# The output-weight requests of a recurrent-memory kernel: from two queues to one, two of them earlier

## The chip, the cores and the metric

The kernel runs on one core of one Trainium2 chip. The metric is the device time of one execution, in microseconds (us). A core has a matrix engine (TensorE, PE in the profile; PEld is its weight load), a vector engine (VectorE, DVE), a scalar engine (ScalarE, ACT), GpSimd (POOL) and SyncE (SP). ACT and SP can both issue transfers (DMA). The instruction that issues one stands in the program of its engine like any other, so what comes after it on that engine starts after it.

## What is computed

Two branches read the same `x` (2048 rows of 512) and are mixed by a gate per row.

```python
# A: 64 segments of 32 rows, one after another; 8 rows of memory pass from each to the next
h = concatenate([mem, xs])                       # 40 rows of 512
q, k, v = h @ Wq, h @ Wk, h @ Wv                 # 32 heads of 128: each weight is 512 x 4096
o = softmax(mask(q @ k.T * scale)) @ v
o = einsum('bhte,hed->btd', o, Wo)               # Wo: 32 heads x 128 x 512
mem, out = o[:8], o[8:]
# B: 4 blocks of 512 rows, 32 heads of 16: causal attention plus a running memory of phi(k) v
# result = g * a + (1 - g) * b,  g = sigmoid((x * gate_w).sum(-1))
```

All inputs are bf16. Wk, Wq, Wv and Wo of branch A have 4 MB each. The segments of A are a recurrence: a segment can't end before its product with Wo, and the next one needs the memory rows from it.

## The kernel before, in words

The program is planned in Python. `Prog` collects, for each engine, a list of instructions in order, with the dependences between them, and `emit` turns these into semaphore waits. An engine runs its list in order. A dependence on a DMA waits for the whole group that the DMA belongs to (`val = 16 * (d.group.base + d.group.count)`, L193): whoever reads Wo waits for all eight of its requests.

There are two stages. The first is the projection of branch B, `b_projections` (L614): 64 pieces, called one after another in the loop of `build` (L371 to L392). Each piece is a product on PE into one bank of PSUM, its eviction by ACT or DVE, and stores of the result to scratch memory in HBM, issued from SP by `store` (L626, issued at L627). The last fourteen pieces, 50 to 63, are those of block 3: keys and queries in turn, a memory product, then four pieces of V (59 to 62), evicted by ACT into `V17` (L679), and a flush. Between the pieces, `plan_loads` hands out requests for the weights of branch A from ACT (L508): twelve of 1 MB, one after each piece n with n % 5 == 2, so the last (of Wv) comes after piece 57. The SP queue holds, in order: the loads of x and of the B weights, then the stores of the pieces as they are made, and a few loads for the attention of B.

`wo_load(q)` (L518) requests heads 4q to 4q+3 of Wo: 512 KB in 512 rows of 1 KB. There are eight. In the kernel before, four come from ACT, after pieces 58, 59, 60 and 61, and four from SP after the last piece:

```python
        if n in (58, 59, 60, 61):
            v.wo_load(n - 58)
    for q in range(4, 8):
        v.wo_load(q)
```

The place of Wo in SBUF held `x` before (`v.x_sb = v.Wo_sb[:, 0:NTT, :]`, L291), so the first four requests also wait for the transposes that read x, which end at 33 us.

The second stage is `plan_a` (L933): 64 segments in groups of four. Before the first one come the eight units of `left_units(0)` (L988), which project the last 8 rows of each of four segments: KL, QL and VL in two halves each (PE at L966), an eviction and a transpose by ACT and DVE, then two turns back on PE (L1022). Then `segment(0)`: Q, K and V (L966), scores, softmax and the product with V (L1211 to L1287), and `wo` (L1302), which calls `out_part` (L1038; PE at L1044), the first reader of Wo. The order inside a segment is written out by hand in `A_ORDER` (L914). Attention of B, loads for it and the tails (mixing and output) fill the gaps. `wob_load` (L523) requests the output weights of B, woB, in eight pieces of 64 KB from SP, planned in segment 1; with nothing to wait for, SP issues them right after Wo.

The evictions of V in the pieces 59 to 62 stand on ACT between the Wo requests. The banks that they free are those into which the first products of `left_units(0)` go.

Of the kernel before, what the change touches and what calls it, by code (L numbers as in the profile page):

```python
# [220 lines left out]
def bass_gated_mix__memory_aug_recurrent_mem_tr__memory_aug_infini_attn__prompt_kernel(  # L221
    nc, A_x, A_mem0, A_Wq, A_Wk, A_Wv, A_Wo, A_seg_len, B_x, B_wq, B_wk, B_wv, B_wo, B_beta, gate_w, out, dbg=None,
):
    with ExitStack() as es:
        build(nc, es, A_x, A_mem0, A_Wq, A_Wk, A_Wv, A_Wo, B_wq, B_wk, B_wv, B_wo, B_beta, gate_w, out, dbg)


def build(nc, es, A_x, A_mem0, A_Wq, A_Wk, A_Wv, A_Wo, B_wq, B_wk, B_wv, B_wo, B_beta, gate_w, out, dbg=None):
    v = NS()
# [86 lines left out]
    def Rs(name):  # L316
        if name not in R:
            R[name] = Res(name)
            home = v.home(name)
            if home:  # L320
                R[name].readers = over(home)
        return R[name]
# [48 lines left out]
    for n in range(len(pieces)):  # L371
        if n in (8, 20, 32):
            x_chunk(v, (n + 4) // 12)
        if n == 9:
            sigmoid(v, v.beta_sb[:, :], v.gB_sb, v.omgB_sb, "gB", [Rs("beta")])
            for src, dst, res in ((v.gB_sb, v.gBp, "gB"), (v.omgB_sb, v.omgBp, "omgB")):
                for j in range(4):
                    q = slice(32 * j, 32 * j + 32)
                    P.op("gp", lambda g, src=src, dst=dst, q=q, j=j: g.tensor_copy(dst[q, :], src[q, :].rearrange("p (f j) -> p f j", j=4)[:, :, j]),
                         reads=[Rs(res)], writes=[Rs(res + "p")], name="%sp%d" % (res, j))  # L380
            v.late_const()
        if n >= 36 and n % 2 == 0 and gates:
            gates.pop(0)()
        pieces[n]()
        if n == len(pieces) - 3:
            v.late_mask()
        if n in (36, 38, 40, 42):
            bat.load(0, n // 2 % 2, "kv"[n // 40])
        if weights and n % 5 == 2:
            weights.pop(0)()  # L390
        if n in (58, 59, 60, 61):
            v.wo_load(n - 58)  # L392
    for q in range(4, 8):
        v.wo_load(q)


# [87 lines left out]
def plan_loads(v, A_x, A_mem0, A_Wq, A_Wk, A_Wv, B_wq, B_wk, B_wv, B_wo, B_beta, gate_w):  # L484
    P, Rs, C, M = v.P, v.Rs, v.C, v.M
    xsrc = A_x[0].rearrange("(i p) d -> p i d", p=128)

    def ld(grp, dst, src, res, name):
        P.dma(P.group(grp), lambda s: s.dma_start(dst, src), writes=[Rs(res)], name=name)

    def x(k):
        for h in range(2):
            o = 4 * k + 2 * h
            ld("x%d%d" % (k, h), v.x_sb[:, o:o + 2, :], xsrc[:, o:o + 2, :], "x_sb%d%d" % (k, h), "dma_x%d%d" % (k, h))
    x(0)
    for nm, dst, src in (("wk", v.wkB, B_wk), ("wq", v.wqB, B_wq), ("wv", v.wvB, B_wv)):
        ld("b" + nm, dst[:, :, :], src.rearrange("(c p) n -> p c n", p=128), nm + "B", "dma_" + nm)
    x(1)
    g = P.group("small")
    for fn, res in ((lambda s: s.dma_start(v.beta_sb[:, :], B_beta.rearrange("(o n) -> o n", o=1).to_broadcast([128, v.HB])), "beta"),  # L500
                    (lambda s: s.dma_start(v.gwr_sb[0:C, :], gate_w.rearrange("(c p) -> c p", p=128)), "gwr"),
                    (lambda s: s.dma_start(v.mem0_sb[0:M, :], A_mem0[0]), "mem0")):
        P.dma(g, fn, writes=[Rs(res)], name="dma_" + res)
    x(2)
    x(3)

    def weight(grp, dst, src, res, c):
        P.dma(grp, lambda s: s.dma_start(dst[:, c, :], src[c * 128:(c + 1) * 128].rearrange("p h e -> p (h e)")),  # L508
              writes=[Rs(res)], name="dma_%s%d" % (res, c), eng="act")
    pend = []  # L510
    for res, dst, src in (("Wk", v.Wk_sb, A_Wk), ("Wq", v.Wq_sb, A_Wq), ("Wv", v.Wv_sb, A_Wv)):
        grp = P.group(res)
        for c in range(C):
            pend.append(lambda grp=grp, dst=dst, src=src, res=res, c=c: weight(grp, dst, src, res, c))
    grp = P.group("Wo")
    wosrc = v.A_Wo.rearrange("h e d -> e h d")

    def wo(q):  # L518
        P.dma(grp, lambda s: s.dma_start(v.Wo_sb[:, 4 * q:4 * q + 4, :], wosrc[:, 4 * q:4 * q + 4, :]),
              writes=[Rs("Wo")] + ([Rs("x_sb%d%d" % (q, h)) for h in range(2)] if q < 4 else []), name="dma_Wo%d" % q, eng="act" if q < 4 else "sp")  # L520
    v.wo_load = wo

    def wob():  # L523
        grp = P.group("bwo")
        rows = B_wo.rearrange("(f g j d) n -> g j d f n", f=C, g=2, j=4)
        for j in range(4):
            for g in range(2):
                o = 32 * j + 16 * g
                P.dma(grp, lambda s, j=j, g=g, o=o: s.dma_start(v.woB_sb[o:o + 16, :, :], rows[g, j]), writes=[Rs("woB")], name="dma_woB%d%d" % (j, g))
    v.wob_load = wob  # L530
    return pend


def x_chunk(v, k):

    P, Rs, BK, C = v.P, v.Rs, v.BK, v.C
    for h in range(2):
        bk = BK.take()
        tiles = (4 * k + 2 * h, 4 * k + 2 * h + 1)

        def f(pe, bk=bk, tiles=tiles):
            ins = None
            for n, i in enumerate(tiles):
                for c in range(C):
                    o = (n * C + c) * 128
                    ins = pe.transpose(v.pb16[bk][:, o:o + 128], v.x_sb[:, i, c * 128:(c + 1) * 128], v.ident[:, :])
            return ins
        P.op("pe", f, reads=[Rs("x_sb%d%d" % (k, h)), Rs("ident")], writes=[v.rbank[bk]], name="xtr%d_%d" % (k, h))
        t0 = 128 * tiles[0]
        dst = v.xT[:, :, t0:t0 + 256].rearrange("p c (n t) -> p n c t", t=128)  # L550
        src = v.pb16[bk][:, 0:1024].rearrange("p (n c t) -> p n c t", n=2, c=C)
        for n in range(2):
            v.evac("dve" if h else "act", dst[:, n, :, :], src[:, n, :, :], [bk], [Rs("xT%d_%d%d" % (k, h, n))], "xev%d_%d%d" % (k, h, n))
        BK.give(bk)
# [6 lines left out]
def sigmoid(v, src, g, o, res, reads):  # L561

    P, rg = v.P, v.Rs(res)
    P.op("act", lambda a: a.activation(g[:, :], src, ACT.Exp, scale=-1.0), reads=reads, writes=[rg], name=res + "_e")
    P.op("dve", lambda d: d.tensor_scalar(g[:, :], g[:, :], 1.0, None, op0=ALU.add), reads=[rg], writes=[rg], name=res + "_a")
    P.op("dve", lambda d: d.reciprocal(g[:, :], g[:, :]), reads=[rg], writes=[rg], name=res + "_r")
    P.op("dve", lambda d: d.tensor_scalar(o[:, :], g[:, :], -1.0, 1.0, op0=ALU.mult, op1=ALU.add), reads=[rg], writes=[v.Rs("om" + res)],
         name="om" + res)
# [906 lines left out]
```

## Time and profile before

| | us |
|---|---|
| median of 3 runs | 927.47 |
| lowest, highest | 926.53, 928.67 |
| the profiled execution: its own time | 927.84 |
| its span, first to last instruction | 926.1 |
| busy: PE, DVE, ACT, POOL | 856.1, 651.3, 590.7, 247.1 |
| DMA: moved in all | 51.36 MB |
| DMA rate in the first three 40ths of the span | 333, 403, 372 GB/s |

The profile is one execution; its time is that of the span and of what lies around it. "Busy" is the time in which at least one instruction of the engine runs. In a timeline, SPq and ACTq are the sequencers of SP and ACT issuing a DMA; the length beside such a line is the time that issuing took, not that of the transfer. The time to landing is counted from the issue. A bracket such as `[4.27 <-ACT V L357]` says that the engine was idle for 4.27 us before this instruction and that an ACT instruction writing V at line 357 ended it; `<-issue` means that nothing the profile shows ended it. The granted clock (PEclk) is 1.00 when PE has its full clock.

### The profile page before, as it was taken

Reading aid. Unit: us, or ns where it says so; the run is one execution under the profiler, and the core shown is the slowest. Engines: PE = TensorE matmul, PEld = TensorE weight load, DVE = VectorE, ACT = ScalarE, POOL = GpSimd, SP = SyncE. Lnnn points to the kernel's source line nnn. Section 1 sums busy time; section 2 is a strip of 40 time slices with the busy share of each in tenths; the row PEclk is TensorE's granted clock in tenths of the full one; section 3 lists DMA queues with packets and bytes.
Section 4 is the critical chain, followed back from the end, with each engine's and each line's share of the span. In section 5 each row is a group of like instructions: output and inputs, shape, how many; then the busy total and the mean of one; then the engine's idle time right before and its main releaser. Section 6 shows DMA issues by size and latency. Waiting matters only on the chain. (4 is left out here: it accounts for less than half of the span.)

```text
span 926.1 us, 51464 instructions
## 1 busy us (share of the span) xinstructions
PE 856.1 (92%) x23047; PEld 442.0 (48%) x23054; DVE 651.3 (70%) x1505; ACT 590.7 (64%) x1287; POOL 247.1 (27%) x556
## 2 busy tenths in 40 slices
PE   8979989998999999999999999999999989999886
PEld 4534444444444444444445454544454445444443
DVE  4745757676676868677677777767677777868664
ACT  5745667666666676666666666666666666666453
POOL 3601222222222322223222232223322232222110
PEclk9999999999999999999999999999999999999999
DMA  9996000000011011101011111100011101000010
GB/s 333 403 372 186 13 12 17 25 12 18 16 22 43 23 44 33 33 6 28 19 20 37 28 48 33 27 15 21 22 33 39 39 21 44 17 21 4 26 44 19
DMA packets 63813, 51.36 MB, mean 55 GB/s; under 512 B 34272, under 2 KB 60008, under 8 KB 62056
## 3 DMA queue, kind: packets, MB, share of 16 engines
q1 hardware_dynamic: 59752, 33.38, 12.9%
q10 hardware_dynamic: 3840, 14.68, 4.1%
q8 instruction: 181, 2.97, 1.3%
q14 instruction: 40, 0.33, 0.1%
HBM read 33.47 MB, written 14.57 MB: 52 GB/s over the span
## 5 line engine op out<-in xcount | busy, mean ns | idle before, releaser
L818 ACT ACTIVATE PT<-ps 128x1024 bf16<-128x1024 f32 x160 | 163.2, 1020 | 32.4 <-PE ps L804 31.4
L825 POOL TENSOR_SCALAR_AFFINE_SELECT PT<-PT 128x512 bf16<-128x512 bf16 (+1 forms) x96 | 75.8, 789 | 265.9 <-ACT PT L818 255.8
L966 PE MATMUL ps<-Wv_sb,hT 128*32 128x512 bf16 x2048 | 139.2, 379 | 0.0
L966 PE MATMUL ps<-Wq_sb,hT 128*32 128x512 bf16 x2048 | 136.2, 380 | 1.3 <-ACT hT L357 0.8
L966 PE MATMUL ps<-Wk_sb,hT 128*32 128x512 bf16 x2048 | 135.4, 379 | 0.0
L1044 PE MATMUL ps<-Wo_sb,OT_sb 128*32 128x512 bf16 x2048 | 122.1, 380 | 0.0
L1265 POOL TENSOR_TENSOR P_sb<-P_sb,R_sb 128x64 bf16<-128x64 bf16 x128 | 53.6, 419 | 236.5 <-PE ps L1219 130.8
L357 ACT ACTIVATE OT_sb<-ps 128x320 bf16<-128x320 f32 x192 | 76.7, 434 | 52.5 <-PE ps L1287 38.4
L359 DVE CAST V_sb<-ps 128x512 bf16<-128x512 f32 x128 | 87.7, 685 | 24.1 <-PE ps L966 19.9
L978 DVE STREAM_TRANSPOSE QT_sb<-QN_sb 128x256 f32<-128x256 f32 x128 | 56.3, 440 | 50.5 <-ACT QN_sb L357 50.2
L357 ACT ACTIVATE QN_sb<-ps 128x512 bf16<-128x512 f32 x128 | 77.0, 601 | 21.5 <-PE ps L966 19.4
L966 PEld LDWEIGHTS ps<-Wk_sb,hT 128*32 128x32 bf16 x2048 | 53.9, 97 | 52.8 <-issue 2.3
L359 DVE CAST WH<-ps 128x256 bf16<-128x256 f32 x128 | 53.7, 420 | 31.7 <-PE ps L1044 29.7
L1228 ACT ACTIVATE P_sb<-ps 128x224 bf16<-128x224 f32 x128 | 45.7, 357 | 40.8 <-DVE QT_sb L978 17.5
L1044 PEld LDWEIGHTS ps<-Wo_sb,OT_sb 128*32 128x32 bf16 x2048 | 50.3, 96 | 44.5
L966 PEld LDWEIGHTS ps<-Wq_sb,hT 128*32 128x32 bf16 x2048 | 47.9, 96 | 47.8 <-ACT hT L357 15.5
L978 DVE STREAM_TRANSPOSE KT_sb<-KN_sb 128x256 f32<-128x256 f32 x128 | 56.1, 438 | 15.5 <-ACT KN_sb L357 13.0
L1252 ACT ACTIVATE R_sb<-ps 128x160 f32<-128x160 f32 x128 | 39.0, 305 | 40.9 <-PE ps L1245 40.9
L804 PE MATMUL ps<-QTj,KTj 32*128 32x256 bf16 (+1 forms) x768 | 62.3, 254 | 1.3 <-ACT aT_st L357 1.3
L1259 DVE TENSOR_TENSOR P_sb<-P_sb,R_sb 128x160 bf16<-128x160 bf16 x128 | 42.4, 332 | 29.8 <-ACT R_sb L1255 18.5
L1275 PE MATMUL ps<-P_sb,V_sb 32*128 32x40 bf16 x2048 | 35.3, 178 | 30.1 <-DVE P_sb L1259 14.1
L357 ACT ACTIVATE LN_sb<-ps 128x512 bf16<-128x512 f32 (+1 forms) x96 | 50.4, 525 | 13.6 <-DVE LN_sb L1055 8.8
(136 smaller groups left out, 1552.5 us busy)
## 6 DMA issues: line engine op xcount, KB each, us to landing
Wk_sb<-in_A_Wk_dram ACTq DMA_DIRECT2D x4, 1024.0 KB, 8.2
scr_kqd<-stgk SPq DMA_DIRECT2D x16, 256.0 KB, 8.7
Wq_sb<-in_A_Wq_dram ACTq DMA_DIRECT2D x4, 1024.0 KB, 7.9
Wv_sb<-in_A_Wv_dram ACTq DMA_DIRECT2D x4, 1024.0 KB, 7.7
scr_vd<-V SPq DMA_DIRECT2D x16, 136.0 KB, 6.6
Vj<-scr_vd SPq DMA_DIRECT2D x32, 68.0 KB, 2.4
Wo_sb<-in_A_x_dram SPq DMA_DIRECT2D x8, 256.0 KB, 6.8
KTj<-scr_kqd SPq DMA_DIRECT2D x128, 16.0 KB, 1.7
```

The source lines that it names most:

```text
L357: P.op("act", lambda a: a.activation(dst, src, ACT.Copy), reads=[v.rbank[k] for k in bks], writes=dres, name=name)
L359: P.op("dve", lambda d: d.tensor_copy(dst, src), reads=[v.rbank[k] for k in bks], writes=dres, name=name)
L804: ins = pe.matmul(v.pb[bks[x]][:, 256 * e + o:256 * e + o + w], KT[e][r, 128 * kc:128 * (kc + 1)], QT[r, q0:q0 + w], start=True, stop=True ...
L818: P.op("act", lambda a: a.activation(pt[:, :, :], v.ps[:, bks[0]:bks[1] + 1, :], ACT.Exp, scale=v.SCALE_B), reads=[v.rbank[b] for b in bks ...
L825: P.op("gp", lambda g: g.affine_select(mv, mv, [[0, mv.shape[1]], [1, 128]], ALU.is_ge, 0.0, base=0, channel_multiplier=-1), reads=[rp], w ...
L966: ins = pe.matmul(pb[bk][SEG * j:SEG * (j + 1), :], lhs(c), cols(w, j) if split else w[:, 512 * j:512 * (j + 1)], start=(c == 0), stop=(c ...
L978: P.op("dve", lambda d: d.transpose(to, src), reads=reads, writes=writes, name=name)
L1044: ins = pe.matmul(pb[bk][SEG * j:SEG * (j + 1), :], lhs(4 * k + j), Wo_sb[:, 4 * k + j, :], start=(first and k == ks[0]), stop=False, skip ...
L1228: P.op("act", lambda a: a.activation(P_sb[:, b, :], pb[bk][:, 0:224], ACT.Exp, scale=SCALE), reads=[rbank[bk]], writes=[Rs("P%d" % b), Rs( ...
L1252: P.op("act", lambda a: a.activation(R_sb[:, b, :], pb[bk][:, 224:384], ACT.Ln), reads=[rbank[bk]], writes=[Rs("R%d" % b)], name="ln%d_%d" ...
L1259: P.op("dve", lambda d: d.tensor_tensor(wide(P_sb, b)[:, :, 0:L], wide(P_sb, b)[:, :, 0:L], R_sb[:, b, :].rearrange("p (i q) -> p i q", q= ...
L1265: P.op(ENG["n"], lambda d: d.tensor_tensor(left(P_sb), left(P_sb), grp04(R_sb[:, b, :]), ALU.mult), reads=[Rs("R%d" % b)], writes=[Rs("P%d ...
```

## The change

All eight requests for Wo come from SP. Two of them are made between the pieces, after pieces 56 and 59; the other six after the last piece. ACT issues none.

```diff
-        if n in (58, 59, 60, 61):
-            v.wo_load(n - 58)
-    for q in range(4, 8):
+        if n in (56, 59):
+            v.wo_load((n - 56) // 3)
+    for q in range(2, 8):
         v.wo_load(q)
...
     def wo(q):
         P.dma(grp, lambda s: s.dma_start(v.Wo_sb[:, 4 * q:4 * q + 4, :], wosrc[:, 4 * q:4 * q + 4, :]),
-              writes=[...], name="dma_Wo%d" % q, eng="act" if q < 4 else "sp")
+              writes=[...], name="dma_Wo%d" % q)
```

`P.dma` issues from SP unless told otherwise. In SP's order the first request stands between the store of the third query piece of block 3 (issued at 58.96 us before) and the next store (60.67); the second stands after the store issued at 63.20 and before the last three stores of V. The other six follow the last store of V, and the eight requests of woB follow them.

## The prediction

> **What bounds the kernel now.** I first read two rows of the page: its 40 slices, 23.2 us each, of PE (TensorE) and of the DMA engines.
>
> ```profile
> PE   8979989998999999999999999999999989999886
> ...
> DMA  9996000000011011101011111100011101000010
> ```
>
> DMA is full in the first 80 us and nearly idle afterwards, and PE is full almost everywhere. So from the first segment on the program is a dense chain on PE, and a shift of its start carries to the end. Only the first 85 us can be changed by moving weight requests; all eight output-weight requests go out there. Next I read the timeline from 60 to 90 us, engine by engine (columns: start, length, engine, line, operation; in brackets the idle time before it and what ended it).
>
> ```profile
> 61.78 0.60 ACT L357 ACTIVATE V<-ps 128x512 bf16<-128x512 f32 x1
> 61.86 0.82 ACTq L519 DMA_DIRECT2D Wo_sb<-in_A_Wo_dram  x1
> 62.73 0.60 ACT L357 ACTIVATE V<-ps 128x512 bf16<-128x512 f32 x1 [0.35 <-issue]
> 62.81 3.71 ACTq L519 DMA_DIRECT2D Wo_sb<-in_A_Wo_dram  x1
> 66.57 0.60 ACT L357 ACTIVATE V<-ps 128x512 bf16<-128x512 f32 x1 [3.24 <-issue]
> 67.06 0.59 ACT L357 ACTIVATE LN_sb<-ps 128x512 bf16<-128x512 f32 x1
> ...
> 67.22 3.61 PE L966 MATMUL ps<-Wq_sb,xL 128*32 128x512 bf16 x32 [4.27 <-ACT V L357]
> 70.60 3.11 PE L966 MATMUL ps<-Wv_sb,xL 128*32 128x512 bf16 x32
> ...
> 85.18 1.91 PE L1044 MATMUL ps<-Wo_sb,OT_sb 128*32 128x512 bf16 x32
> ```
>
> See three things. ScalarE (ACT) issues the fourth Wo request for 3.71 us; the last eviction of V stands behind it; PE waits 4.27 us for the bank which that eviction frees. Then 32 matmuls of QL take 3.61 us where 32 of the same form at 85.18 take 1.91. The third thing is the first use of Wo, at 85.18, with no wait in front of it. The windows view explains the slow matmuls (columns: stretch, length, then busy time of PE, PEld, DVE, ACT, POOL, granted clock, DMA share, GB/s):
>
> ```profile
> 62.81:66.22 3.41, 0.14 (x4) 0.00 (x0) 1.54 (x4) 0.52 (x1) 0.00 (x0) 1.00 1.03 353
> 66.22:69.64 3.42, 2.42 (x24) 0.95 (x28) 0.45 (x1) 1.50 (x3) 0.00 (x0) 0.50 1.07 383
> 69.64:73.05 3.41, 3.41 (x36) 1.31 (x32) 0.89 (x2) 1.17 (x3) 0.00 (x0) 0.50 1.09 380
> 73.05:76.46 3.41, 2.37 (x65) 1.20 (x61) 2.28 (x4) 0.81 (x2) 0.97 (x3) 1.00 1.10 363
> ```
>
> After a stretch of 3.41 us with 0.14 us of work, PE ran at half clock for 6.83 us. DMA stayed full all the while. Last, the answer on Wo_sb, cut to the last of SyncE's (SP's) four Wo requests:
>
> ```profile
> L519 SPq DMA_DIRECT2D Wo_sb<-in_A_Wo_dram x1: 2831/2831/2831, 69.5 to 69.5; - x1
> ...
> DMA to landing us min/median/max: 13.1/13.1/13.1
> ```
>
> It was issued at 69.48 and landed 13.1 later, at 82.6. So the first product with Wo has 85.2 - 82.6 = 2.6 us of slack on the transfer. That slack is the heart of the matter.
>
> **What the Trainium skill says.** "DMA: Bandwidth & Descriptors", section "Issuing engines are not separate DMA queues": requests from ACT and SP run on the same 16 engines, and issuing from several saves only issue time. The trace agrees: 383 GB/s with requests of both, against 340 to 363 at 6 to 10 us, when SP's queue was alone. The same page, "Queues, rings and completion order": each engine takes turns between queues, packet by packet; this trace's windows don't show the turns. "TensorE: Matmul & The Clock Gate", "Part 1": the clock halves after an idle window of about 3.4 us, which runs free of the kernel; the trace shows 0.50 over 6.83 us, two such windows.
>
> **The change, part by part.**
>
> *Removed: four requests from ACT.* ACT's queue of four V evictions starts at 61.25 (it waits there for an earlier store of V, which stays). Two that nothing separates start 0.53 apart (61.25, 61.78), so the fourth starts at 61.25 + 3 x 0.53 = 62.84 and ends at 63.44. QL starts at about 63.5, not 67.22. PE's gap is then 0.55 us, so I take the clock as full: QL's 32 matmuls last 1.9, to 65.4. What is late next is Wv: its last request, at 59.23, landed 7.7 later, at 66.9. VL starts at 67.0 instead of 70.60. From there at full clock: first half's result 1.05 (the shape's duration at 75.38), ACT eviction 0.65 with its start, DVE transpose 0.45, DVE eviction of the second half 0.69, its transpose 0.45, then the step to Q of segment 0 (75.38 - 75.16 = 0.22). Sum 3.5, to 70.6, where before it was 75.38: 4.8 us earlier. Everything from Q to the first use of Wo (9.8 us) is computation and moves with it: 85.2 - 4.8 = 80.4. This is when PE asks for Wo.
>
> *Added: four requests on SP, six of the eight after the pieces.* Issue cost first. SP is free between 59.67 and 60.67, so the first of the two inserted (0.4 to 0.7 us each) is free; the second comes after the store at 63.20 and pushes three V stores back 0.7 us. Their readers come after 85 us or later, and each store has at most 1 MB of Wo ahead of it: 2.8 us at 380 GB/s, added to the landing of the last store (67.19 and 6.4, 73.6). Nothing waits; were a reader to need one before 76.4, it would cost that difference.
> How the ring fills: 3 requests of 512 packets (512 KB in rows of 1 KB) went out in 0.39 to 0.82 us each, and the fourth blocked, on ACT 3.71 and on SP 2.83. SP will block likewise from the fourth outstanding request on. Behind it on SP are only more Wo, the eight woB requests (not used before the first tail) and the loads at 101.65. I cost the blocking at nothing: the transfer engines are fed by what fills the ring. Without that cover, an empty queue, each us of blocking would be a us of landing.
>
> *Moved: when the last Wo lands.* Bytes and packets are the same and DMA is full throughout, so the landing moves only with the rate. From 66 to 74 both queues gave 382 to 388, in the mean 383 GB/s: 3.07 MB. One queue with 1 KB packets gave 363 and 340 (6 to 10 us) and, mostly alone, 349 and 322 (76 to 80); I take 352 for it. 3.07 MB then take 8.7 instead of 8.0 us, 0.7 more; some 0.2 comes back at 60 to 66 us, where the queue now holds more than small stores (332 to 366 GB/s). Last landing: 82.6 + 0.5 = 83.1. Bounds: 0.5 us earlier than before (a full queue with no mixing) to 2.5 later (303 GB/s, the slice 10 to 12 us).
>
> *The new wait.* PE asks at 80.4 and gets at 83.1. Behind the waiting instruction on PE stand all of W, the next scores and the fills; ACT and DVE soon run dry. So the shift of the whole chain isn't 4.8 but 85.2 - 83.1 = 2.1 us.
>
> *The clock again.* The new gap is about 2.7 us. A 3.41 us stretch with 0.93 busy at the end of the kernel (919.56) was followed by 0.50; one with 1.96 busy (878.60) kept 1.00. So some idle share between 1.45 and 2.48 us decides; I take 2.0. With a free phase, a gap of 2.7 puts over 2.0 into one stretch in (3.41 - 2.7 + 2 x 0.7) / 3.41 = 0.62 of executions. Each then runs at least one stretch at half clock: 1.7 us, two of them 3.4. I charge 0.62 x 1.7 = 1.0. Bounds 0 and 3.4.
>
> *Sum.* The profiled execution took 927.84 us, its span 926.1 and 1.7 around it; 927.84 - 2.1 + 1.0 = **926.7 us**. The median of the runs, 927.47, lies 0.4 below that execution, so this is only 0.8 under the median.
>
> **Rivals.** 0.2% is 1.9 us, about what a measurement of this kernel can tell from no change: the borders are 925.6 and 929.3.
> A, forecast: Wo's landing takes the place of the ACT stall, and the clock falls in part of the executions; 925.6 to 928.9. For it: slack of 2.6 against a gain of 4.8. Chance 0.57.
> B, the same, but the landing is up to 0.7 us earlier than I say or the clock never falls: 927.84 - 2.1 to 2.9, about 925.3. For it: 1.96 busy kept the clock. Chance 0.24.
> C, Wo is there at 80.4: 927.84 - 4.8 = 923.0. Against it: 512 KB need 1.4 us, and two would have to be saved. Chance 0.04.
> D, slower: SP's single queue is too slow. Some 5.1 MB have to move from 66 us to the last landing, less 2.6 for the tail of the slowest engine seen before (14.0 us before). At 303 GB/s it is 16.9, landing 85.5; the gap of 5 us then surely halves the clock for one or two stretches, on average 2.5 us: 927.84 + 0.3 + 2.5, about 930.6. With one sure stretch (1.7) it passes zero from a landing at 83.5 on, which is below 344 GB/s. For it: 322 at 78 to 80; against it: 340 to 363. Chance 0.11.
> E, the stall isn't removed, since the eviction waits for something else too: 927.6. Against it: its bracket says issue. Chance 0.04.
>
> **The numbers.** Faster: B and C, 0.28. Same: A and E, 0.61. Slower: D, 0.11. The range leaves out C, the far end of B and the upper half of D: 924.7 to 929.8.
>
> **What would show it.** Right: no Wo request on ACT; the fourth V eviction near 62.8 and QL near 63.5 with clock 1.00; VL released by Wv near 67; PE idle in front of the first L1044 from about 80.4 to 83; a last Wo landing near 83. The clock column after 83 says whether A or B holds. Wrong: L1044 starts without a wait (C), it starts after 85 (D), or the gap before QL stays (E).

## The result and the profile after

| | before | changed |
|---|---|---|
| median (runs) | 927.83 (4) | 927.85 (4) |
| lowest, highest | 926.53, 928.67 | 926.1, 929.14 |
| profiled execution, span | 927.84, 926.1 | 929.14, 927.4 |

The ratio is 1.000, 95% interval 0.9979 to 1.0021. A second measurement with more rounds (experiment 11) gave 0.9999, 0.9978 to 1.0019. The change makes no difference that can be measured. The ratios leave out executions in which the chip was in a slower state; the medians are of all.

The two rows of the page look as before:

```profile
PE   8987989998999999999999999999999989999886
...
DMA  9996000000011011101011111100011111000010
```

The timeline of the changed kernel shows what moved (ACT first, then PE, then the SP sequencer):

```profile
62.08 2.07 ACT L357 ACTIVATE V<-ps 128x512 bf16<-128x512 f32 x4 [0.16 <-DMA scr_vd<-V]
...
64.20 1.91 PE L966 MATMUL ps<-Wq_sb,xL 128*32 128x512 bf16 x32 [0.25 <-ACT V L357]
67.66 1.91 PE L966 MATMUL ps<-Wv_sb,xL 128*32 128x512 bf16 x32 [1.55 <-DMA Wv_sb<-in_A_Wv_dram]
...
84.45 3.31 PE L1044 MATMUL ps<-Wo_sb,OT_sb 128*32 128x512 bf16 x32 [3.71 <-DMA Wo_sb<-in_A_Wo_dram]
...
67.93 7.54 SPq L519 DMA_DIRECT2D Wo_sb<-in_A_Wo_dram  x6
```

The four V evictions now follow each other, the gap of 4.27 us ahead of QL is 0.25, and QL takes 1.91 us instead of 3.61. PE is free for Wo at 80.74; before it used Wo at 85.18. But a new bracket stands at L1044: 3.71 us of waiting for Wo, and the product then takes 3.31 us instead of 1.91. The windows view says why (same columns as before):

```profile
66.00:68.00 2.00, 0.45 (x12) 0.23 (x12) 0.88 (x2) 0.60 (x1) 0.00 (x0) 1.00 1.07 380
70.00:72.00 2.00, 1.26 (x45) 0.83 (x49) 1.36 (x3) 0.60 (x1) 0.68 (x3) 1.00 1.08 382
80.00:82.00 2.00, 0.74 (x32) 0.20 (x21) 1.16 (x3) 1.22 (x4) 0.33 (x1) 1.00 1.20 228
82.00:84.00 2.00, 0.00 (x0) 0.00 (x0) 0.45 (x1) 0.09 (x1) 0.73 (x3) 1.00 0.70 120
81.39:84.80 3.41, 0.35 (x8) 0.23 (x12) 0.45 (x1) 0.70 (x2) 1.06 (x3) 1.00 0.71 130
84.80:88.21 3.41, 3.41 (x40) 1.15 (x28) 0.42 (x1) 0.00 (x0) 0.00 (x0) 0.50 0.04 11
```

A stretch with 0.35 us of work is followed by one at half clock, as before, only 18.6 us later. Two more things are in these rows. SP's queue moves 382 GB/s at 70 to 72 us, where it is alone (the last Wv request of ACT has landed at 67.6). And at the end, from 80 us, the rate is 228 and then 120 GB/s while the engines' busy share is 1.20 and 0.70. The answer on Wo_sb, cut to the last request:

```profile
L519 SPq DMA_DIRECT2D Wo_sb<-in_A_Wo_dram x1: 1422/1422/1422, 74.0 to 74.0; - x1
...
DMA to landing us min/median/max: 10.4/10.4/10.4
```

It lands at 84.4, against 82.6 before. Now the end: the product starts 0.7 us earlier than before (84.45 for 85.18), ends 0.7 later (87.75 for 87.09), and in segment 1 the same product stands 0.9 later. It stands 1.0 later in the last segment and 0.8 to 1.1 in those between, so up to there nothing after 90 us adds or gives back more than 0.2. Part of the 0.9 is no effect of the change: in this execution the projection was already late before any changed instruction (the last Wv request, unchanged in the program, at 60.19 instead of 59.23).

So the place to compare is the end of the first product with Wo. From there to the end of the span it was 839.0 us before and 839.6 in the changed kernel; in the experiments with one semaphore for Wo it was 838.9 to 840.2.

### The profile page after: what moved, and what is told of

It is laid out like the page before. It is cut to its first block, busy times and chain, and to the rows that moved or that the text cites. A ratio compares the mean times of both kernels' runs of the same rounds, so it can differ in the third digit from the quotient of the medians.

```text
span 927.4 us, 51467 instructions
## 1 busy us (share of the span) xinstructions
PE 856.2 (92%) x23054; PEld 442.3 (48%) x23054; DVE 650.3 (70%) x1505; ACT 590.2 (64%) x1287; POOL 246.0 (27%) x556
## 5 line engine op out<-in xcount | busy, mean ns | idle before, releaser
L1044 PE MATMUL ps<-Wo_sb,OT_sb 128*32 128x512 bf16 x2048 | 123.5, 383 | 3.7 <-DMA Wo_sb<-in_A_Wo_dram 3.7
L359 DVE CAST V_sb<-ps 128x512 bf16<-128x512 f32 x128 | 87.6, 685 | 23.8 <-PE ps L966 19.6
L1044 PEld LDWEIGHTS ps<-Wo_sb,OT_sb 128*32 128x32 bf16 x2048 | 50.6, 97 | 48.9 <-DMA Wo_sb<-in_A_Wo_dram 3.8
```

The source lines that it names most:

```text
L359: P.op("dve", lambda d: d.tensor_copy(dst, src), reads=[v.rbank[k] for k in bks], writes=dres, name=name)
L1044: ins = pe.matmul(pb[bk][SEG * j:SEG * (j + 1), :], lhs(4 * k + j), Wo_sb[:, 4 * k + j, :], start=(first and k == ks[0]), stop=False, skip ...
```

## The experiments

All were timed beside the kernel before; the median of that kernel was 927.94 beside experiments 1 to 4, 927.07 beside 5 to 8 and 927.48 beside 9 to 11. To take out how early the projection ran, I also count the last completion of Wo from the last Wv request: 23.3 us before, 24.2 in the changed kernel, 23.5 in its second profiled execution (experiment 11). Each of these is one execution, so a difference of 0.7 us here can be chance.

My theory was that the landing of the last Wo had become the bound, and that the clock paid for the wait. The rivals: SP's single queue is slow; the gain comes and is given back in the segments; the ACT stall was not from the fourth request.

**1. Three requests on ACT, the fourth on SP.**

```diff
-        if n in (58, 59, 60, 61):
+        if n in (58, 59, 60):
             v.wo_load(n - 58)
-    for q in range(4, 8):
+    for q in range(3, 8):
...
-eng="act" if q < 4 else "sp"
+eng="act" if q < 3 else "sp"
```

> Three requests stay on ACT after pieces 58, 59 and 60; the fourth moves to the head of SP's five. Theory (the ACT stall comes from the fourth request alone; behind it the landing of the last Wo is the bound): no Wo request on ACT takes over 1 us, QL starts near 63.5 us with clock 1.00, PE waits for Wo in front of the first L1044, last landing 82.5 to 84.5; time within 0.2% of before. Rival (SP's single queue moves Wo slower than two): with two queues again the last landing is 1 us or more earlier than the 84.4 of the changed kernel, and the time 925.5 to 926.5. Rival (three requests block ACT as well): a gap of 3 us or more before QL stays.

Ratio 0.9993 (0.9967 to 1.002). ACT and PE of this kernel:

```profile
63.31 0.65 ACTq L519 DMA_DIRECT2D Wo_sb<-in_A_Wo_dram  x1
64.01 1.09 ACT L357 ACTIVATE V<-ps 128x512 bf16<-128x512 f32 x2 [0.17 <-issue]
...
84.38 2.40 PE L1044 MATMUL ps<-Wo_sb,OT_sb 128*32 128x512 bf16 x32 [2.91 <-DMA Wo_sb<-in_A_Wo_dram]
```

No request on ACT takes over 0.65 us and the gap before QL is 0.64: without the fourth request there is no stall. With both queues in use, the last Wo completes at 84.3, 23.8 after the last Wv request, between the two executions of the changed kernel. The slow single queue falls, as the rate of 382 had said.

**2. The changed kernel, woB later.** The eight woB requests wait for the last PE instruction planned in segment 0.

```diff
     def wob():
         grp = P.group("bwo")
+        last = P.ops["pe"][-1]
...
-writes=[Rs("woB")], name=
+writes=[Rs("woB")], deps=[last], name=
```

> The changed kernel, with the eight woB requests waiting for the end of segment 0 on PE. Theory (the last Wo request shares the engines with woB at its end: the eighth landing came 3.55 us after the seventh in the changed kernel, 1.5 between the others): the eighth lands 1.3 to 2 us after the seventh, PE's wait in front of the first L1044 shrinks from 3.7 to 1.5 to 2.3, time 925 to 926.5. Rival (woB stands behind Wo in the same queue and costs it nothing): last landing and wait stay, time 927.8.

Median 926.3, ratio 0.9984 (0.9966 to 1.0002), which just fails to exclude no difference. PE and the windows of the profiled execution (924.34 us):

```profile
81.25 1.91 PE L1045 MATMUL ps<-Wo_sb,OT_sb 128*32 128x512 bf16 x32 [1.18 <-DMA Wo_sb<-in_A_Wo_dram]
```

```profile
78.00:80.00 2.00, 2.00 (x68) 0.85 (x60) 1.36 (x3) 0.87 (x3) 0.45 (x1) 1.00 0.71 228
80.00:82.00 2.00, 0.82 (x28) 0.42 (x20) 0.94 (x3) 1.25 (x3) 0.87 (x3) 1.00 0.05 16
```

Compare the first of these rows with the changed kernel at 80 to 82: the same 228 GB/s, but a busy share of 0.71 instead of 1.20. With woB in the queue, the engines are busy and move little. The last completion is 22.5 after the last Wv request, 1.7 and 0.9 sooner than in the two executions of the changed kernel, the wait is 1.18 and the clock stays full.

**3. The changed kernel, one semaphore for each Wo request,** so that each part of the product waits for its own two.

```diff
-    grp = P.group("Wo")
+    grps = [P.group("Wo%d" % q) for q in range(8)]
...
-        P.dma(grp, ...
-              writes=[Rs("Wo")] + ...
+        P.dma(grps[q], ...
+              writes=[Rs("Wo%d" % q)] + ...
...
-reads=reads + [Rs("Wo")],
+reads=reads + [Rs("Wo%d" % k) for k in ks],
```

> The changed kernel, with a semaphore for each Wo request, so that each part of the product waits for its own two requests. Theory (the wait for the whole group is what took the gain): the first L1044 starts at about 80.6 without a wait for Wo, 24 of 32 matmuls run before the last landing and only the last 8 wait for it; the product ends 0.5 us after the landing instead of 1.9 (3.3 at half clock), the clock stays 1.00; time 925 to 926.5. Rival (the gain is given back in the segments that follow): the product ends earlier, time unchanged at 927.8.

Median 926.72, ratio 0.9996 (0.9978 to 1.0013). The profiled execution was a long one (935.64 us: the clock fell twice in the projection), but its order is as planned:

```profile
87.71 1.48 PE L1044 MATMUL ps<-Wo_sb,OT_sb 128*32 128x512 bf16 x24
91.75 0.61 PE L1044 MATMUL ps<-Wo_sb,OT_sb 128*32 128x512 bf16 x8 [2.56 <-DMA Wo_sb<-in_A_Wo_dram]
```

24 matmuls run without a wait, the last 8 wait. Yet the ratio doesn't show the 1.4 us expected. In this kernel it was 841.6 us from the end of the product to the end of the span, some 2 more than elsewhere: PE waits 1.7 us for a load of oTg at L1135 near 348 us, where the kernel before doesn't. Experiment 7 has such a wait too (1.33). Why eight semaphores bring it about is open.

**4. The wait filled with matmuls.** 11 matmuls into an unused bank ahead of the first product.

```diff
+            if first and s == 0:
+                ... 11 x pe.matmul(pb[bk], xT[:, 0, 0:128], xT[:, 0, 0:512], start=True, stop=True)
```

> The changed kernel, with 11 matmuls of 128x512 into an unused bank on PE ahead of the first product with Wo (added work, 2.4 us, which lies in the wait). Theory (the wait of 3.7 us halves the clock behind it, worth 1.6 us in the profiled execution): the wait left is 0.5 to 2 us, the granted clock stays 1.00 after it, the 32 matmuls of L1044 last 1.9 us; time about 1 us under the changed kernel, 926.5 to 927.2. Rival (the clock's fall has another cause or costs nothing): time unchanged at 927.8 or longer by up to 0.5.

```profile
81.36 2.55 PE L1311 MATMUL ps<-xT 128*128 128x512 bf16 x11
85.65 1.91 PE L1044 MATMUL ps<-Wo_sb,OT_sb 128*32 128x512 bf16 x32 [1.74 <-DMA Wo_sb<-in_A_Wo_dram]
```

The clock stayed at 1.00 and the product took 1.91: with the wait filled, the clock doesn't fall in this execution. The ratio, 1.0007 (0.9987 to 1.0026), shows no gain: in this execution Wo landed at 85.6. Whether the half clock costs 1 us on average stays unshown; what it costs in one execution, and when it comes, is seen below.

**5. The kernel before, woB later** (the edit of 2).

> The kernel before, with the eight woB requests waiting for the end of segment 0. Theory (in the kernel before, the ACT stall is the bound and Wo lands in its slack): the fourth Wo request on ACT still blocks for 3 us or more, the gap before QL stays, the first L1044 starts at its own time without a wait for Wo although the last Wo lands 1 us or more earlier; time within 0.2% of before. Rival (the woB requests cost time in their own right, whatever the stall): as much gain as in the changed kernel, 1.5 us (926.3).

Ratio 1.0003 (0.9979 to 1.0028). ACT and PE:

```profile
64.37 4.04 ACTq L519 DMA_DIRECT2D Wo_sb<-in_A_Wo_dram  x1
68.46 0.60 ACT L357 ACTIVATE V<-ps 128x512 bf16<-128x512 f32 x1 [3.57 <-issue]
...
85.61 1.91 PE L1045 MATMUL ps<-Wo_sb,OT_sb 128*32 128x512 bf16 x32
```

The stall is there, Wo completes at 83.5 (22.7 after the last Wv request), 2.1 us before PE asks. That is 0.6 sooner than in the kernel before, not the 1 us or more that I had expected, and it is worth nothing here. The bound is the stall, as the page of the kernel before had said.

**6. The changed kernel without four of the eight requests.** Half of the heads then use what lay in Wo's place before; the matmuls are the same.

```diff
-        if n in (56, 59):
-            v.wo_load((n - 56) // 3)
-    for q in range(2, 8):
+    for q in range(4, 8):
         v.wo_load(q)
```

> The changed kernel without the requests for heads 0 to 15 of Wo, so that the product of half of the heads uses the wrong operand (2 MB less to load; the matmuls are the same). Theory (only the landing of Wo holds back the 4.8 us): PE finds Wo landed at about 80.5 us less or more the shift of the projection, no wait in front of L1044, clock 1.00; time 923 to 924. Rival (the gain is given back by the segments that follow): no wait either, but time 926.5 to 928.

Median 923.75, ratio 0.997 (0.9952 to 0.9989).

```profile
79.18 0.19 PE L1285 MATMUL ps<-P_sb,VL 32*128 32x64 bf16 x4
79.30 1.91 PE L1042 MATMUL ps<-Wo_sb,OT_sb 128*32 128x512 bf16 x32
```

No wait, full clock, and the gain stays to the end: 838.9 us from there. That refutes "given back later". The ratio says 2.8 us, with an interval from 1.0 to 4.5 us; the 4.8 expected from one profiled execution lies just outside.

**7. Experiments 2 and 3 together.**

> The changed kernel with a semaphore for each Wo request and with woB waiting for the end of segment 0. Theory: the first L1044 starts without a wait at about 80.5, the last eight matmuls wait for at most 0.5 us, clock 1.00; nearly all of the 4.8 us show: time 923 to 924.5, ratio 0.995 to 0.997 of before. Rival (the two cures overlap, or the gain is given back): 926 to 927.

Median 925.09, ratio 0.9975 (0.996 to 0.999): faster than before by 0.25%, less than expected. The profiled execution was not a typical one (929.47):

```profile
79.46 1.05 PE L1045 MATMUL ps<-Wo_sb,OT_sb 128*32 128x512 bf16 x16
80.89 0.61 PE L1045 MATMUL ps<-Wo_sb,OT_sb 128*32 128x512 bf16 x8 [0.38 <-ACT LN_sb L357]
85.10 0.84 PE L1045 MATMUL ps<-Wo_sb,OT_sb 128*32 128x512 bf16 x8 [3.60 <-DMA Wo_sb<-in_A_Wo_dram]
```

Of the 16 completions of the last request, 15 came by 81.80 and one at 84.96. The request before it was held back in the same way, 15 by 80.47 and one at 83.64. What held these two back is open.

**8. All eight requests after the last piece.**

```diff
-        if n in (56, 59):
-            v.wo_load((n - 56) // 3)
-    for q in range(2, 8):
+    for q in range(8):
```

> The changed kernel with all eight requests after the last piece, none between the pieces. Theory (transfers are full either way, so the order among Wo and the stores of block 3 matters by the bytes that pass ahead): the V stores land 1 MB earlier, the last Wo lands within 1 us of the 84.4 of the changed kernel, PE waits for it; time within 0.2% of the changed kernel. Rival (the two early requests are what keeps the queue full): the last landing is 2 us or more later, time 929 to 930.

Ratio 1.0027 (1.001 to 1.0045): slower, against my expectation.

```profile
85.63 3.61 PE L1042 MATMUL ps<-Wo_sb,OT_sb 128*32 128x512 bf16 x32 [4.30 <-DMA Wo_sb<-in_A_Wo_dram]
```

Wo completes 25.9 us after the last Wv request, 1.7 and 2.4 later than in the two executions of the changed kernel. One thing that I had left out is the order: 1 MB of Wo lost its place ahead of the last three stores of V, and these 0.4 MB (1.1 us) now pass first, for the first request some earlier stores too. The rival isn't excluded for the rest. The engines moved 335 to 352 GB/s at 60 to 66 us (332 to 366 in the kernel before), but at 68 to 72 us only 296 and 317, against 378 and 382 in the changed kernel: 0.29 MB, 0.8 us. Why is open: experiment 2, with the early requests in place, moved 318 at 70 to 72. So the two early requests matter, at least in part for what they overtake; experiments 9 and 10 try that part.

**9. Wo ahead of the last V stores, woB later** (with the edit of 2).

```diff
-        if n in (56, 59):
-            v.wo_load((n - 56) // 3)
-    for q in range(2, 8):
-        v.wo_load(q)
+        if n == 56:
+            v.wo_load(0)
+        if n == 59:
+            for q in range(1, 8):
+                v.wo_load(q)
```

> The changed kernel with woB waiting for the end of segment 0, and with the last seven Wo requests all after piece 59, ahead of the last three stores of V (0.4 MB, 1.1 us at 375 GB/s). Theory (what passes ahead of the last Wo, and woB beside its end, set its landing): the last Wo lands about 21.4 us after the last Wv request (24.2 in the changed kernel, 22.5 with woB late alone), PE waits for it for at most 0.5 us in front of the first L1044, the clock stays 1.00; time 1 us under the kernel with woB late alone, 924 to 925.5, ratio 0.995 to 0.998. Rival (blocked stores of V hold back someone): a new wait on a store of V in the first segments, time over 926.

Median 923.69, ratio 0.9969 (0.9956 to 0.9982).

```profile
81.00 1.91 PE L1046 MATMUL ps<-Wo_sb,OT_sb 128*32 128x512 bf16 x32 [0.61 <-DMA Wo_sb<-in_A_Wo_dram]
```

**10. The same order, woB where it was.**

> The same order of Wo ahead of the last V stores, woB as in the changed kernel. Theory: the V stores now stand between Wo and woB, so woB starts later as well; the last Wo lands 22 to 23.5 us after the last Wv request, PE's wait is 1 to 2.5 us, time 925.5 to 927. Rival (only woB beside the end matters): last landing 24 or more after the last Wv request, time 927 to 928.

Median 923.97, ratio 0.9966 (0.995 to 0.9982).

```profile
80.58 1.91 PE L1045 MATMUL ps<-Wo_sb,OT_sb 128*32 128x512 bf16 x32 [0.54 <-DMA Wo_sb<-in_A_Wo_dram]
```

Wo completes 21.3 and 21.2 us after the last Wv request in 9 and 10, about 3.0 and 2.2 sooner than in the two executions of the changed kernel; PE never waits for the late V stores in the first segments, and the clock stays full. Experiment 10 did better than I expected: with the V stores between Wo and woB, holding woB back adds nothing. It is the changed kernel with nothing but an order of requests altered, and it beats both kernels by 0.3%.

**11. The changed kernel again.**

> The changed kernel itself once more, with more rounds beside the kernel before. Theory (gain and new wait cancel): ratio 0.999 to 1.001; PE waits 2.5 to 4 us for Wo in front of the first L1044, with the clock at 0.50 afterwards in this execution or not. Rival (a real loss or gain within the first interval): a ratio off 1 by more than 0.001 with an interval that leaves 1 out.

Ratio 0.9999 (0.9978 to 1.0019). The wait for Wo was 3.22 us, the clock fell again behind it, the product took 2.90.

## Why the prediction was right, and where its sizes were off

**The stall and its removal: right.** The fourth eviction, QL, VL's wait for Wv and the first segment came as worked out. I said 63.5 for QL, 67.0 for VL, 70.6 for Q of segment 0 and 80.4 for the request of Wo (my terms behind VL add up to 70.5, not 70.6); measured 64.20, 67.66, 71.34 and 80.74, in an execution whose projection ran about 1 us later. Experiment 1 shows that without the fourth request the stall is gone.

**The new wait takes the gain: right.** The bracket at L1044 names Wo. Experiment 6 takes the wait away by loading less and the gain appears; 9 and 10 do it with everything loaded; 5 shows that the same cure does nothing where the stall bounds.

**The landing: right in size by luck, wrong in its cause.** I forecast 83.1, which is 23.9 after the last Wv request; measured 24.2 and, in experiment 11, 23.5. But I had charged 0.7 us to a single queue with 1 KB packets, at 352 GB/s, although I had just cited that the requests of ACT and SP run on the same engines. SP's queue alone moved 378 to 382 GB/s at 68 to 74 us, where both had moved 380 to 384 (from 66 on 380 to 388; I had read 382 to 388), and 346 to 364 at 74 to 80, where 322 to 354 had moved before: that term is about zero. The rates that I took it from (6 to 10 us, 76 to 80) belong to their stages, not to the number of queues. (My bound of 2.5 us at 303 GB/s is 2.1 by the same 3.07 MB; nothing rests on it.)

What took its place stands at both ends. At 62 to 64 us, with Wv beside little else, 295 GB/s moved against 366 before: 0.14 MB, 0.4 us; in experiment 11 it was 359, and its landing is 0.7 sooner. And the end is slower: from the completion count 112 of 128 (each request counts 16) to the last one it was 2.86 us before and 3.55 in the changed kernel (3.00 in experiment 11). Where woB or the V stores came later, it was 1.68 to 2.31 (experiments 2, 5, 9, 10); where woB stood right behind Wo, 2.86 to 4.80 (before, the changed kernel, 1, 4, 8, 11), but only 2.20 in 6. Experiment 2 shows that woB there costs the landing. Part of this cost (0.6 us by experiment 5) was in my starting point, where woB stood behind Wo too; I never asked whether it was there or would grow.

**The ring: right in its price, with one omission.** SP's six requests took 0.79 to 1.53 us each, 7.54 in all, without one stall of 3 us, and nobody missed the time. But I treated the place of the two early requests as free of consequence for the landing. Experiment 8 shows that it is worth 1.7 to 2.4 us, and 9 and 10 that more of the same is worth nearly the whole wait.

**The clock: the mechanism was right.** One stretch at half clock followed the wait in both profiled executions of the changed kernel. From the start of the product to the next fill on PE it was 3.90 us (84.45 to 88.35) against 2.28 before (85.18 to 87.46): 1.6, where I had put 1.7 for one stretch. I charged it to 0.62 of executions; two of two had it, which doesn't settle the share. The waits were longer than my 2.7 us, 3.71 and 3.22, in part because the way from Q of segment 0 to the request took 9.40 us instead of 9.80. For such waits my own reckoning gives 0.91 and 0.77 of executions, so some 1.3 to 1.5 us instead of 1.0 (an estimate).

The idle share that I had guessed at 2.0 us can be read from all thirteen profiled executions together. The falls of the clock lie on one grid of 3.413 us: in the kernel before, 66.22 and 922.97 are 251 steps apart. I take every stretch of that grid from 5 us on that ran at full clock and has a whole stretch behind it. In 11 of them PE worked 1.43 us or less, and each was followed by half clock; in the other 3458 it worked 1.46 us or more, and each was followed by full clock. The two nearest cases, from experiment 8 and then experiment 4:

```profile
79.90:83.31 3.41, 1.43 (x56) 0.63 (x53) 2.15 (x5) 1.69 (x4) 1.27 (x4) 1.00 1.00 227
83.31:86.73 3.42, 1.10 (x12) 0.46 (x16) 0.00 (x0) 0.00 (x0) 0.14 (x1) 0.50 0.19 46
...
66.58:69.99 3.41, 1.46 (x29) 0.66 (x28) 0.89 (x2) 0.72 (x2) 0.00 (x0) 1.00 1.07 379
69.99:73.41 3.42, 2.28 (x64) 1.20 (x60) 2.16 (x4) 1.07 (x2) 0.97 (x3) 1.00 1.09 383
```

So in these runs a stretch with about 1.95 us of idle time or less was safe. Of the waits for Wo, all from 2.91 us up were followed by half clock (experiments 1, 7, 8, 11 and the changed kernel), none up to 2.56 (2, 3, 4, 9, 10).

**The sum.** I expected 926.7 from 927.84 - 2.1 + 1.0. By the same steps with measured sizes: Wo lands 24.2 (23.5) instead of 23.3 us after the last Wv request, so about 0.5 us later; the shift is 2.6 - 0.5 = 2.1, less 1.6 for the clock, and 0.5 of gain is left, which a measurement with an interval of 0.2% doesn't see. The forecast's 1.1 is in the same case. The unchanged time alone would also have fitted a change that does nothing; it is the traces and experiments 6, 9 and 10 that show a gain and a loss cancelling.

## What to carry to other kernels

A request that blocks its engine is found by the bracket behind it; what its removal is worth is the slack of the next late thing, here 2.6 us of 4.8, minus what the new wait does to the clock. Here, with transfers at full rate, choosing the queue moved nothing; what landed in time was decided by what stood ahead in the order and by what small transfers stood behind it. So ask of each store whether someone needs it before the weight behind it.

## What the runs showed of the hardware that was not expected

- SP's queue alone, with packets of 1 to 2 KB, reached 378 to 382 GB/s at 68 to 74 us, as much as SP and ACT together (380 to 384).
- The eight woB requests, 64 KB each into 16 partitions, kept the engines busy beyond their share (1.20) at 228 GB/s; transfers of Wo at the same rate took a share of 0.71. Whether the 16 partitions are the reason was not tried.
- A fourth outstanding Wo request of 512 packets blocked its issuer for 3.71 and 4.04 us on ACT and for 2.83 on SP. The count alone doesn't decide: in experiment 1 the third of SP's five took 2.94, and in experiment 6 SP issued four in 0.51 to 1.27 us each before the first had landed. In both cases on ACT, the stall ended (66.52 and 68.41) just before the last Wv request, ahead in the same queue, landed (66.94 and 68.75). What fills the queue was not tried.
- In thirteen executions, PE's clock halved after every stretch of the 3.41 us grid with 1.43 us of work or less, and after none with 1.46 or more.
